# Attention units laid out anew: score bursts, value products, whole-array work and row-half pairs in separate runs

## The chip, the cores and the metric

The kernel runs on one core of one Trainium2 chip. The metric is the device time of one execution in microseconds. A core has TensorE (PE, with its weight loads as PEld), VectorE (DVE), ScalarE (ACT), GpSimd (POOL) and SyncE (SP), which issues most of the DMAs. TensorE writes to PSUM, which has eight banks of 128 x 512 float32 here; GpSimd does not read PSUM in this kernel.

## What is computed

Four layers on one sequence of 2048 rows of width 512, each with a layer norm ahead of it and a residual sum behind it: Fourier mixing, memory attention, Fourier mixing, memory attention.

```
x = x + A(layernorm(x));  x = x + B(layernorm(x));  x = x + A(layernorm(x));  x = x + B(layernorm(x))
A: real part of DFT_seq(DFT_hidden(x)), by given DFT matrices
B: q, k, v = x@wq, x@wk, x@wv  in 32 heads of 16;  four segments of 512 rows, one after the other:
     p = softmax(q k' * scale + causal mask);  a_dot = p v
     phi(t) = t + 1 if t > 0 else exp(t)
     a_mem = (phi(q) M) / (phi(q) z + 1e-6)
     o = g * a_mem + (1 - g) * a_dot,   g = sigmoid(beta) per head
     M += phi(k)' v;  z += sum phi(k)
   result: o @ wo
```

## The kernel before

Every matmul input that needs more than one pass's precision is split in a high and a low part (`split`, L99 to L107: high by ScalarE, low by VectorE or GpSimd), and three passes are summed (`matmul3`). `place_spectral` writes the Fourier layers, `place_attention` the attention layers.

**The order of the work is written out by hand.** Generators are placed on a line of slots: `place(order, gen, times...)` says that the next piece of `gen` runs at each of these times; pieces of the same time run by `order`. All pieces are then issued in that order. TensorE keeps it to the letter (`keep_in_program_order`; its matmuls all stand on L86 of the profile). On the other engines a scheduler orders the instructions by priority; tiles come from pools with a number of buffers (`bufs`), and an instruction that needs a buffer waits until one is free. All PSUM tiles share eight banks (`bank`).

**A unit** is four heads of one segment (`HU` = 4): eight units a segment, 32 an attention, 64 in all. A unit has ten slots; unit n starts at t = t0 + 10 n. The pieces, with their slot in the old layout counted from t (a time of t - 17 is slot 3 of the unit two before):

- `stack` (t - 22): four DMAs on SP (L893) copy q and k of the unit's heads from DRAM (`scrq`, `scrk`) into `stkq` and `stkk`, two heads side by side on the row halves 0 to 63 and 64 to 127. `stkq` has three buffers, and `stkk` is one of three tiles used in turn, so a copy goes over what the unit three before has used last.
- `natural_max` (t - 17, -15, -13, -11, -9, and t - 8): scores in natural order (`nat`, 48 rows on each half of the array), whose row maxima VectorE takes by a fused add-mask-and-minimum (L925, output `junk`); then the maxima are split into `mparts`.
- `max_rows` (t - 5): two transposes (`mT`), two copies by ScalarE (`mt`), two DMAs into spare rows of `stkq` (L963).
- `softmax_values` (t to t + 8): five score bursts, transposed (`sT`, 50 rows on each half): `third` at 0, the two `second` at 2 and 4, the two `first` (512 columns) at 6 and 8. ScalarE rectifies the diagonal blocks (L996) and takes the exponential into `pT` (L999), two of each a burst; GpSimd then zeroes what lies above the diagonal (`affine_select`, L1002).
- `value_products` (t + 11.9): 16 matmuls of 128 rows and 32 columns (`pv_bank`, 32 records of the profile), and a copy by ScalarE (`ot`, L1064).
- `output` (mostly t + 21.9): four transposes (`on`, whole array), a reciprocal, the multiplication (L1105, two halves) and the addition to `o_nat` by GpSimd (L1107).

**Segment items** run on the whole array: `prep` (normalise and transpose rows of the next segment, `xnT` to `xT`; `xn` has two buffers), `transpose_out` (`oT` to `oh`), `mem_read` (`pm`), `mem_update` (transposes `pkT`, a copy `pkn` by ScalarE, then `pM`). `apart(s, k)` puts them at slot 1.9 of the segment's unit k, beside `output` and ahead of `value_products`.

**The chain** holds projections (`pqk`), values (`pvv`) and the output projection (`po`): each tile is 12 products, each done as two half products of 64 rows on the two halves of the array. `chain_step(k)` issues step k of the first half of one tile and step k - `LAG` of the second half of an earlier one, so that two matmuls run side by side (a pair of row halves). A unit holds two tiles, 24 steps, spread evenly:

```
LAG = STEPS * 3 // 2                                     # STEPS = 12
chain_time(k) = t0 + 5 * (k // STEPS) + 2.2 + 4.6 * (k % STEPS) / (STEPS - 1)
```

A tile's second half starts when a score burst behind its first half has been read out of PSUM (`evicted`). `chain_tail` follows the last step: for a projection two copies by ScalarE (`praw`, `parts`), the difference by GpSimd (L855), for phi a rectification and an exponential by ScalarE and a sum by VectorE (`feature_sum`, L851), and two slots later the writes to `scrq` or `scrk` (L869).

Of the kernel before, what the change touches and what calls it, by code (L numbers as in the profile page):

```python
# [19 lines left out]
P = 128  # L20
# [22 lines left out]
HALF = NT // 2  # L43
URGENT = 150
TERMS = {
    "P1": (((0, 1), None, None),),
# [13 lines left out]
def spectral_infini_kernel(  # L60
# [135 lines left out]
    def finish(ps, xr, x_out, i):  # L196
# [5 lines left out]
    spare = v_all.rearrange("p a b -> p (a b)")[:, : 6 * 512].rearrange("p (a b) -> p a b", b=512)  # L202
    v_count = [0]
    max_parts = [
        consts.tile([P, MCOLS], F32R, name=f"mparts{i}") for i in range(2)
# [500 lines left out]
    def place_attention(x_in, x_out, t0, w_at, out_at):  # L706
# [93 lines left out]
        STEPS = DT * len(PASSES)  # L800
        LAG = STEPS * 3 // 2

# [30 lines left out]
        def keep_proj(s, g, n, ps):  # L833
            def phi_tile():
                if (s, g) not in phi:
                    phi[s, g] = pair("phi", "ut", 8, F32)
                return phi[s, g][:, "qk".index(n)]

            parts = sb.tile([P, 2, 512], F32R, name="parts", bufs=2)
            with_phi = (n == "q" and s > 0) or (n == "k" and s < NSEG - 1)  # L840
            late = s == 0 and g < 2
            raw = sb.tile([P, 512], F32, name="praw", bufs=2)
            sign = -1.0 if n == "q" else 1.0

            def feature():
                A.activation(phi_tile(), raw, AF.Relu, scale=-sign)
                A.activation(phi_tile(), phi_tile(), AF.Exp, scale=-1.0)

            def feature_sum():
                op = (ALU.min, ALU.subtract) if n == "q" else (ALU.max, ALU.add)  # L850
                V.scalar_tensor_tensor(phi_tile(), raw, 0.0, phi_tile(), op0=op[0], op1=op[1])  # L851

            A.activation(raw, ps, AF.Copy, scale=sign)
            A.activation(parts[:, 0], ps, AF.Copy, scale=sign)
            G.tensor_tensor(out=parts[:, 1], in0=raw, in1=parts[:, 0].bitcast(F32), op=ALU.subtract)  # L855
# [44 lines left out]
        def natural_max(s, g, u):  # L900
# [3 lines left out]
            def scores(*cols):  # L904
# [16 lines left out]
                for k, (src, dst) in enumerate(views[::2] + views[1::2]):  # L921
                    n = src.shape[1]
                    junk = sb.tile([P, 512], BF16, name="junk", bufs=1)
                    with tc.high_priority(offset=URGENT):
                        last_max[0] = V.tensor_tensor_reduce(  # L925
                            junk[:, :n], src, mask[:, 512 - n :], 1.0, 3e38,
                            ALU.add, ALU.min, dst,
                        )
# [40 lines left out]
        def softmax_values(s, g, u):  # L969
# [60 lines left out]
            for p in range(HP):  # L1030
# [13 lines left out]

                ev(6 + 2 * p, first)
                ev(2 + 2 * p, second)
            p2 = []
# [6 lines left out]

            ev(0, third)

# [10 lines left out]
            pending[s, g, u] = last  # L1067
            for t in range(9):
                for f in events.get(t, ()):
                    f()  # L1070
# [8 lines left out]
        def output(s, g, u):  # L1079
# [16 lines left out]
            for j in range(0, LT, 2):  # L1096
# [180 lines left out]
        def apart(s, k):  # L1277
            return t0 + SS * s + SU * k + 1.9

        for n in range(NSEG * USEG):  # L1280
            t = t0 + SU * n
            final = n >= NSEG * USEG - 2
            place(0, softmax_values(*unit(n)), run_from(t, 9))
# [3 lines left out]
            turn = t - (6 if x_out is out_tiles and n == NSEG * USEG - 1 else 5)  # L1287
            place(1.9, max_rows(*unit(n)), [turn])
            place(1, natural_max(*unit(n)), run_from(t - 17, 5, 2), [t - 8])
            place(0.6, stack(*unit(n)), [t - 22])  # L1290
        for s in range(NSEG):
            b = t0 + SS * s
            for j in range(2):
                t = b - 43 + 5 * j if s == 0 else apart(s - 1, 2 + j)
                first = (12, 10, 6, 4, 3) if s == NSEG - 1 else (11, 8, 5, 3) if s else (8, 5, 4, 3)
                place(0.4, prep(s, (2 * j, 2 * j + 1)), [*(t - d for d in first), t, t + 1] if s == 0 else [*(t - d for d in first), t])
# [4 lines left out]
            order = [chain_proj(s, 3, n) for n in "qk"]  # L1301
            order += [chain_out(s - 1, i) if s else None for i in range(LT)]
# [3 lines left out]
            if s < NSEG - 1:  # L1306
                order += [chain_proj(s + 1, g, n) for g in range(2) for n in "qk"]
                order += [chain_values(s + 1, i) for i in range(2)]
                order += [chain_proj(s + 1, 2, n) for n in "qk"]
                order += [chain_values(s + 1, i) for i in (3, 2)]  # L1310
            chain.update({at + h: tile for h, tile in enumerate(order) if tile})
# [14 lines left out]
            for g in range(NG):  # L1326
# [21 lines left out]
        for j in chain:  # L1348
            end = chain_time(STEPS * (j + 1) - 1 + LAG) + 0.05
            place(2.1, chain_tail(j), [end, end + 1, end + 1.5, end + 2] if chain[j].name == "pqk" else [end])  # L1350
# [110 lines left out]
```

## Time and profile before

| | |
|---|---|
| median of three runs | 1838.15 us (1837.44 to 1843.29) |
| profiled execution | 1843.37 us, span 1841.7 us |
| granted TensorE clock | 0.981 |
| first attention, value products | from 478 to 953 us of the span |
| second attention, value products | from 1384 to 1831 us |

The profile's parts: busy time by engine; groups of instructions (line, engine, operation, output<-input, count, then busy us, mean ns of one, and the idle time before them with what ended it); waits (engine, line, what it waited for: us in total, times, longest); windows (busy time of each engine, with counts, in stretches of the span); the timeline (start in us, time, instructions in order). A matmul's record is longer than its share of the array, since matmuls overlap in the pipe: the pace is read from start to start.

### The profile page before, as it was taken

The page shows a single profiled execution, that of the slowest core. Times are in us where ns is not written, and L with a number is a line of the kernel's source. Part 1 is how long each engine was busy: PE and PEld are TensorE (multiplying, and loading weights), DVE is VectorE, ACT ScalarE, POOL GpSimd, SP SyncE. Part 2 cuts the span into 40 slices and gives each one's busy share as a digit, 9 for nine tenths or more (in the row PEclk, how much of TensorE's full clock was granted, in tenths as well). Part 3 has the DMA queues.
Part 4 walks back from the last instruction along what each step waited for, and adds up shares of the span by engine and source line. Part 5 has one row for each costly group of instructions (what it writes and reads, how often), then busy time and mean ns, then how long its engine had stood idle before and what let it go on. Part 6 is the DMA issues. An engine that isn't in the chain of part 4 may idle for free. (4 is left out here: it accounts for less than half of the span.)

```text
span 1841.7 us, 35419 instructions
## 1 busy us (share of the span) xinstructions
PE 1751.0 (95%) x11504; PEld 1332.9 (72%) x11504; DVE 1389.4 (75%) x4114; ACT 1076.4 (58%) x2452; POOL 362.8 (20%) x673
## 2 busy tenths in 40 slices
PE   8999999999999999999899999999999999989998
PEld 6888777877666666666578878888876667667665
DVE  8888987764766878878867997667457677787784
ACT  3344434441777777677664675453337877767765
POOL 1000000002332333334410000000222333333332
PEclk9999999999899999999799999999998999999988
DMA  7787764354543545544556776645535455455450
GB/s 283 248 268 243 238 222 160 126 166 161 156 132 91 154 124 134 144 123 126 159 189 213 260 237 227 195 134 161 177 117 158 122 134 145 122 133 145 100 133 25
DMA packets 145512, 303.30 MB, mean 165 GB/s; under 512 B 18096, under 2 KB 22192, under 8 KB 145328
## 3 DMA queue, kind: packets, MB, share of 16 engines
q1 hardware_dynamic: 138416, 288.44, 52.8%
q10 hardware_dynamic: 6912, 12.59, 1.8%
q8 instruction: 93, 1.52, 0.4%
q14 instruction: 91, 0.75, 0.1%
HBM read 211.83 MB, written 88.08 MB: 163 GB/s over the span
## 5 line engine op out<-in xcount | busy, mean ns | idle before, releaser
L925 DVE CUSTOM_DVE_ANT_0 junk<-nat,mask 128x512 bf16<-128x512 f32 (+3 forms) x1024 | 499.7, 488 | 172.9 <-PE nat L86 93.9
L999 ACT ACTIVATE pT<-sT 128x512 f32<-128x512 f32 x640 | 354.4, 604 | 0.6 <-POOL pT L1002 0.2
L86 PE MATMUL m<-chi,xa 128*128 128x512 f32 x1056 | 308.7, 392 | 3.1 <-DVE c L549 2.1
L1002 POOL TENSOR_SCALAR_AFFINE_SELECT pT<-pT 128x256 f32<-128x256 f32 (+1 forms) x448 | 195.0, 450 | 513.8 <-ACT pT L999 298.5
L86 PE MATMUL m<-clo,xa 128*128 128x512 f32 x720 | 231.1, 393 | 4.7 <-DVE clo L103 4.4
L86 PEld LDWEIGHTS m<-chi,xa 128*128 128x128 f32 x1056 | 198.0, 189 | 47.5 <-DVE c L549 2.9
L86 PE MATMUL sT<-stkq,stkk 50*128 50x256 f32 (+3 forms) x1024 | 196.0, 356 | 21.8 <-ACT pT L999 17.2
L86 PE MATMUL pqk<-xT,wq 64*128 64x512 f32 (+1 forms) x720 | 214.8, 406 | 0.0
L86 PE MATMUL pqk<-xT,wk 64*128 64x512 f32 (+1 forms) x720 | 208.0, 396 | 0.0
L86 PE MATMUL nat<-stkk,stkq 48*128 48x384 f32 (+3 forms) x1024 | 196.8, 344 | 7.9 <-DVE mx L925 2.6
L996 ACT ACTIVATE sT<-sT 128x256 f32<-128x256 f32 x625 | 181.1, 324 | 38.5 <-PE sT L86 35.5
L86 PE MATMUL pvv<-wv,xT 64*128 64x512 f32 (+1 forms) x672 | 192.7, 405 | 0.0
L86 PEld LDWEIGHTS sT<-stkq,stkk 50*128 50x128 f32 x1024 | 118.4, 189 | 99.7 <-ACT pT L999 33.8
L86 PE MATMUL y<-wdt,us 128*128 128x512 f32 x768 | 182.3, 391 | 0.2 <-DVE wdt L103 0.2
L86 PEld LDWEIGHTS y<-wdt,us 128*128 128x128 f32 x768 | 143.4, 188 | 30.4 <-DVE wdt L103 0.9
L86 PE MATMUL pv_bank<-pT,v_all 128*32 128x512 f32 (+3 forms) x2048 | 160.9, 457 | 3.1 <-DVE mx L925 2.0
L86 PEld LDWEIGHTS nat<-stkk,stkq 48*128 48x128 f32 x1024 | 137.2, 191 | 36.6 <-DVE mx L925 10.3
L86 PEld LDWEIGHTS m<-clo,xa 128*128 128x128 f32 x720 | 135.2, 188 | 37.5 <-DVE clo L103 8.9
L86 PE MATMUL po<-wo,oh 64*128 64x512 f32 (+1 forms) x672 | 155.4, 402 | 0.6 <-ACT oh L101 0.5
L101 ACT ACTIVATE chi<-cring 128x512 fp32r<-128x512 f32 (+1 forms) x138 | 99.6, 727 | 87.6 <-PE m L86 36.7
L1064 ACT ACTIVATE ot<-pv_bank 128x512 f32<-128x512 f32 x64 | 38.4, 601 | 191.1 <-PE pv_bank L86 185.5
L86 PEld LDWEIGHTS pqk<-xT,wk 64*128 64x128 f32 (+1 forms) x720 | 121.2, 187 | 7.9 <-issue 2.2
(187 smaller groups left out, 2940.3 us busy)
## 6 DMA issues: line engine op xcount, KB each, us to landing
cring<-in_ct SPq DMA_DIRECT2D x97, 256.0 KB
scrk<-parts SPq DMA_DIRECT2D x96, 256.0 KB
stkq<-scrq SPq DMA_DIRECT2D x128, 192.0 KB
stkk<-scrk SPq DMA_DIRECT2D x128, 192.0 KB
cring<-sum SPq DMA_DIRECT2D x95, 256.0 KB
xt<-mid SPq DMA_DIRECT2D x64, 256.0 KB
scrq<-parts SPq DMA_DIRECT2D x32, 512.0 KB
cring<-in_ct SPq DMA_DIRECT2D x27, 512.0 KB
```

The lines of the kernel that those rows point to most:

```text
L86: return tc.keep_in_program_order(op(*args, **kwargs))
L101: pin(A.activation(hi, src, AF.Copy, scale=scale))
L925: last_max[0] = V.tensor_tensor_reduce(junk[:, :n], src, mask[:, 512 - n :], 1.0, 3e38, ALU.add, ALU.min, dst,)
L996: done = A.activation(blocks, blocks, AF.Relu)
L999: A.activation(dst[a], ps, AF.Exp, scale=-SCALE)
L1002: G.affine_select(blocks, blocks, pattern=[[0, n] for n in blocks.shape[1:-1]] + [[1, P]], compare_op=ALU.is_ge, fill=0.0, base=0, channel ...
L1064: A.activation(ot[:, 0], pb, AF.Copy)
```

## The change

- **Bursts.** The second `second` moves from slot 4 to 3. `natural_max` moves to t - 17.95, -16.05, -13, -12, -10.9 (slots 2.05, 3.95, 7, 8 and 9.1) and t - 9.
- **Chain.** The 24 steps of a unit lie in three runs: nine from slot 4.1, eight from 6.1, seven from 8.1. `LAG` is 19. The tiles have a new order (before: q3 k3 o0 o1 o2 o3 q0 k0 q1 k1 v0 v1 q2 k2 v3 v2); q0, k0 and so on belong to the next segment.
- **Whole-array work.** Segment items move from 1.9 to 2.5, behind the burst of slot 2 and its maxima; `output` moves to t + 12.5 (also 2.5), nearly a unit earlier. Both `prep` of a segment now stand in its unit 2 (before 2 and 3); the two pieces of `mem_update` stand in units (1, 4, 4, 7) and (2, 5, 7, 8), before both in (1, 4, 5, 7); `mem_read` in (0, 2, 3, 6), before (0, 3, 5, 6).
- **Value products** stay at t + 11.9, now between `third` and the burst of slot 2.
- **Features.** GpSimd clamps `raw` in place and adds it; phi of q has its plain sign, so the memory's denominator adds 1e-6.
- **Maxima.** Two instructions in a row write their unused output to different places: a half of `junk`, or back into PSUM.
- **Output.** For s > 0 one multiplication instead of two.

```diff
+S_AT = (0, 2, 3, 6, 8)
+N_AT = (-17.95, -16.05, -13.0, -12, -10.9, -9)
+PV = 11.9
+W = 2.5
+TO = 0.8
+TURNED = (12.5, 12.5, 14)
+WIN = ((4.1, 9), (6.1, 8), (8.1, 7))
+LAGS = 19
+ORDER = "q3 k3 o0 o1 o2 q0 o3 q1 k0 q2 v0 k1 v1 k2 v3 v2"
+OT_AT = (1, 1, 2, 2)
+PREP_AT = (2, 2)
+READ_AT = (0, 2, 3, 6)
+UPA = (1, 4, 4, 7)
+UPB = (2, 5, 7, 8)
...
-        LAG = STEPS * 3 // 2
+        LAG = LAGS
...
             def feature():
                 A.activation(phi_tile(), raw, AF.Relu, scale=-sign)
                 A.activation(phi_tile(), phi_tile(), AF.Exp, scale=-1.0)
+                G.tensor_scalar(raw, raw, 0.0, None, op0=ALU.max if sign > 0 else ALU.min)
             def feature_sum():
-                V.scalar_tensor_tensor(phi_tile(), raw, 0.0, phi_tile(), op0=op[0], op1=op[1])
+                G.tensor_tensor(
+                    out=phi_tile(), in0=phi_tile(), in1=raw, op=ALU.add if sign > 0 else ALU.subtract
+                )
...
-                    junk = sb.tile([P, 512], BF16, name="junk", bufs=1)
+                    trash = src if n == 512 and k else junk[:, :n] if k % 2 == 0 else junk[:, 512 - n :]
...
-                ev(6 + 2 * p, first)
-                ev(2 + 2 * p, second)
+                ev(S_AT[3 + p], first)
+                ev(S_AT[1 + p], second)
...
-                    V.tensor_tensor(out=tmp, in0=num, in1=rb, op=ALU.mult)
+                    if j == 0:
+                        V.tensor_tensor(
+                            out=tmps,
+                            in0=pn[:, :, :, :DH],
+                            in1=rec.unsqueeze(3).to_broadcast([P, LT, HU, DH]),
+                            op=ALU.mult,
+                        )
...
-                V.tensor_scalar_add(dj, pm[:, :, :, DH], -1e-6)
+                V.tensor_scalar_add(dj, pm[:, :, :, DH], 1e-6)
...
-            return t0 + SS * s + SU * k + 1.9
+            return t0 + SS * s + SU * k + W
...
-            place(0.9, value_products(*unit(n)), [t + (12 if final else 11.9)])
-            turned = t + 14 if n >= NSEG * USEG - 3 else t + 14.5 if n % USEG == USEG - 1 else t + 21.9
-            place(0.5, output(*unit(n)), [turned])
+            place(0.9, value_products(*unit(n)), [t + (PVF if final else PV)])
+            turned = t + TURNED[2 if n >= NSEG * USEG - 3 else n % USEG == USEG - 1]
+            place(TO, output(*unit(n)), [turned])
...
-            place(1, natural_max(*unit(n)), run_from(t - 17, 5, 2), [t - 8])
+            place(1, natural_max(*unit(n)), [t + k for k in N_AT])
             place(0.6, stack(*unit(n)), [t - 22])
...
-                t = b - 43 + 5 * j if s == 0 else apart(s - 1, 2 + j)
+                t = b - 43 + 5 * j if s == 0 else apart(s - 1, PREP_AT[j])
...
-                    place(0.1, transpose_out(s - 1, i), [apart(s, 1 + i // 2)])
+                    place(OWO, transpose_out(s - 1, i), [apart(s, OT_AT[i])])
...
-                    place(0.6, mem_read(s, g), [apart(s, (0, 3, 5, 6)[g])] * 2)
+                    place(OWR, mem_read(s, g), [apart(s, READ_AT[g])] * 2)
...
-                    place(0.3, update, [apart(s, (1, 4, 5, 7)[g])])
-                    place(0.7, update, [apart(s, (1, 4, 5, 7)[g])])
+                    place(OWU, update, [apart(s, UPA[g])])
+                    place(OWB, update, [apart(s, UPB[g])])
         def chain_time(k):
-            return t0 + 5 * (k // STEPS) + 2.2 + 4.6 * (k % STEPS) / (STEPS - 1)
+            u, r = divmod(k, 2 * STEPS)
+            for at, n in WIN:
+                if r < n:
+                    return t0 + SU * u + at + 1.8 * r / n
+                r -= n
```

More of the change, by code (lines that the diff above doesn't have):

```diff
@@ L44 @@
 URGENT = 150
+S_AT = (0, 2, 3, 6, 8)
+N_AT = (-17.95, -16.05, -13.0, -12, -10.9, -9)
+PV = 11.9
+PVF = 12
+W = 2.5
+TURN = -5
+TO = 0.8
[8 more added lines that the diff above has]
+UPB = (2, 5, 7, 8)
+OWO = 0.7
+OWU = 0.3
+OWP = 0.3
+OWR = 0.6
+OWB = 0.85
 TERMS = {
@@ L203, in spectral_infini_kernel @@
     v_count = [0]
+    junk = consts.tile([P, 512], BF16, name="junk")
     max_parts = [
@@ L1053, in third @@
                 causal(t[:, :, :P])
-            ev(0, third)
+            ev(S_AT[0], third)
             def last():
@@ L1067, in softmax_values @@
             pending[s, g, u] = last
-            for t in range(9):
-                for f in events.get(t, ()):
+            for t in sorted(events):
+                for f in events[t]:
                     f()
@@ L1282, in place_attention @@
             final = n >= NSEG * USEG - 2
-            place(0, softmax_values(*unit(n)), run_from(t, 9))
-            place(0.9, value_products(*unit(n)), [t + (12 if final else 11.9)])
-            turned = t + 14 if n >= NSEG * USEG - 3 else t + 14.5 if n % USEG == USEG - 1 else t + 21.9
-            place(0.5, output(*unit(n)), [turned])
-            turn = t - (6 if x_out is out_tiles and n == NSEG * USEG - 1 else 5)
+            place(0, softmax_values(*unit(n)), [t + k for k in sorted(set(S_AT))])
+            place(0.9, value_products(*unit(n)), [t + (PVF if final else PV)])
+            turned = t + TURNED[2 if n >= NSEG * USEG - 3 else n % USEG == USEG - 1]
+            place(TO, output(*unit(n)), [turned])
+            turn = t - (6 if x_out is out_tiles and n == NSEG * USEG - 1 else -TURN)
             place(1.9, max_rows(*unit(n)), [turn])
-            place(1, natural_max(*unit(n)), run_from(t - 17, 5, 2), [t - 8])
+            place(1, natural_max(*unit(n)), [t + k for k in N_AT])
             place(0.6, stack(*unit(n)), [t - 22])
@@ L1293, in place_attention @@
             for j in range(2):
-                t = b - 43 + 5 * j if s == 0 else apart(s - 1, 2 + j)
+                t = b - 43 + 5 * j if s == 0 else apart(s - 1, PREP_AT[j])
                 first = (12, 10, 6, 4, 3) if s == NSEG - 1 else (11, 8, 5, 3) if s else (8, 5, 4, 3)
-                place(0.4, prep(s, (2 * j, 2 * j + 1)), [*(t - d for d in first), t, t + 1] if s == 0 else [*(t - d for d in first), t])
+                place(OWP, prep(s, (2 * j, 2 * j + 1)), [*(t - d for d in first), t, t + 1] if s == 0 else [*(t - d for d in first), t])
             if s == 0:
@@ L1300, in place_attention @@
             at = 2 * USEG * s
-            order = [chain_proj(s, 3, n) for n in "qk"]
-            order += [chain_out(s - 1, i) if s else None for i in range(LT)]
             for i in range(LT):
                 if s > 0:
-                    place(0.1, transpose_out(s - 1, i), [apart(s, 1 + i // 2)])
[L1306 to L1310, printed above, removed]
+                    place(OWO, transpose_out(s - 1, i), [apart(s, OT_AT[i])])
+            order = []
+            for name in ORDER.split():
+                n, i = name[0], int(name[1])
+                if n == "o":
+                    order.append(chain_out(s - 1, i) if s else None)
+                elif n == "v":
+                    order.append(chain_values(s + 1, i) if s < NSEG - 1 else None)
+                elif i == 3:
+                    order.append(chain_proj(s, 3, n))
+                else:
+                    order.append(chain_proj(s + 1, i, n) if s < NSEG - 1 else None)
             chain.update({at + h: tile for h, tile in enumerate(order) if tile})
@@ L1348, in place_attention @@
         for j in chain:
-            end = chain_time(STEPS * (j + 1) - 1 + LAG) + 0.05
+            end = chain_time(STEPS * (j + 1) - 1 + LAG) + 0.01
             place(2.1, chain_tail(j), [end, end + 1, end + 1.5, end + 2] if chain[j].name == "pqk" else [end])
```

3 lines of the change are left out of this document (1 added, 2 removed).

## The prediction

> **What bounds the kernel now.** I read the page, then the windows of the value products for the length of a unit, the waits, and the timelines of TensorE and of the DMA queue around one unit.
>
> ```profile
> span 1841.7 us, 35419 instructions
> PE 1751.0 (95%) x11504; PEld 1332.9 (72%) x11504; DVE 1389.4 (75%) x4114; ACT 1076.4 (58%) x2452; POOL 362.8 (20%) x673
> ```
> ```profile
> 520.00:852.00 332.00, 51.51 (x704) 20.09 (x696) 13.18 (x22) 1.00 0.49 128
> 1424.00:1754.00 330.00, 51.94 (x704) 20.28 (x704) 13.18 (x22) 1.00 0.50 129
> ```
>
> TensorE is the one engine that is nearly always busy. The windows count value products alone: 32 records a unit, so 704 are 22 units, of 15.09 and 15.00 us. About 46 units run with a full chain of row-half pairs; the Fourier stages are not touched. One unit on TensorE, with SyncE's issues beside it:
>
> ```profile
> 1604.78 2.36 PE L86 MATMUL pv_bank<-pT,v_all 128*32 128x512 f32 x32
> ...
> 1607.92 0.50 PE L86 MATMUL nat<-stkk,stkq 48*128 48x512 f32 x2
> ...
> 1609.63 0.66 PE L86 MATMUL on<-ident,ot 128*128 128x128 f32 x4
> ...
> 1611.43 0.40 PE L86 MATMUL pqk<-xT,wq 64*128 64x512 f32 x1
> ...
> 1611.67 0.39 PE L86 MATMUL pqk<-xT,wq 64*128 64x512 f32 x1
> ...
> 1613.30 0.52 PE L86 MATMUL sT<-stkq,stkk 50*128 50x512 f32 x2
> ...
> 1616.54 0.39 PE L86 MATMUL pqk<-xT,wq 64*128 64x512 f32 x1
> 1616.86 1.09 PE L86 MATMUL oT<-ident,onat 128*128 128x128 f32 x8
> 1617.80 0.60 PE L86 MATMUL pkT<-ident,phi 128*128 128x128 f32 x4
> 1619.19 1.20 PE L86 MATMUL pM<-v_all,pkn 128*128 128x136 f32 x8 [0.79 <-ACT pkn L1152]
> 1620.31 2.36 PE L86 MATMUL pv_bank<-pT,v_all 128*32 128x512 f32 x32
> 1622.60 0.50 PE L86 MATMUL sT<-stkq,stkk 50*128 50x384 f32 x4
> 1622.94 0.44 PE L86 MATMUL po<-wo,oh 64*128 64x512 f32 x1
> ...
> 1623.46 0.40 PE L86 MATMUL nat<-stkk,stkq 48*128 48x512 f32 x2
> ```
> ```profile
> 1613.74 0.32 SPq L893 DMA_DIRECT2D stkk<-scrk  x1
> ...
> 1615.05 0.41 SPq L893 DMA_DIRECT2D stkk<-scrk  x1
> ```
>
> The sT of 1613.30 is a unit's last score burst (`first`, p = 1). Starts tell the pace: a pair of row halves every 0.24 us (1611.43 to 1611.67), eight transposes in 0.94 (1616.86 to 1617.80, so 0.47 for four), the value products 2.29 (1620.31 to 1622.60), a burst of four score matmuls 0.34 (1622.60 to 1622.94). Where TensorE waits:
>
> ```profile
> PEld sT L86 <- ACT pT L999: 33.8, 45, 1.1
> PEld mT L86 <- ACT pT L999: 24.3, 43, 1.5
> PE sT L86 <- ACT pT L999: 17.2, 30, 0.6
> PE mT L86 <- ACT pT L999: 16.4, 40, 1.3
> PE pM L86 <- ACT pkn L1152: 12.1, 19, 1.8
> ACT ot L1064 <- PE pv_bank L86: 185.5, 56, 5.5
> ```
>
> It waits for a PSUM bank that ScalarE's exponentials still hold, and in `mem_update` for the copy of its own transposes; ScalarE in turn idles 185.5 us, 3 a unit, under the value products. A wait costs more than its row, for the pipe refills: the unit from 1604.78 to 1620.31 took 15.53 us; without its 0.79 (1.1 with the refill), and with 2.1 us of whole-array work in place of its 2.8 (next part), it would take 13.7. So some 1.35 us of each 15.05 are waits, 62 us in 46 units. That is what new places can take away.
>
> **The change part by part.**
>
> *New places.* Before, a unit ran whole-array work, value products, then bursts with pairs spread evenly. Now: third burst (slot 0), value products (1.9), the burst `second` of p = 0 with the first 512-wide maxima (2, 2.05), whole-array work (2.5), the other `second` with maxima (3, 3.95), nine steps of pairs, burst (6), eight steps with maxima between, burst and maxima (8), seven steps with maxima between. The bursts then lie 2.3 to 2.8 us apart, and one asks ScalarE for two rectifications and two exponentials:
>
> ```profile
> L996 ACT ACTIVATE sT<-sT 128x256 f32<-128x256 f32 x625 | 181.1, 324 | 38.5 <-PE sT L86 35.5
> L999 ACT ACTIVATE pT<-sT 128x512 f32<-128x512 f32 x640 | 354.4, 604 | 0.6 <-POOL pT L1002 0.2
> L925 DVE CUSTOM_DVE_ANT_0 junk<-nat,mask 128x512 bf16<-128x512 f32 (+3 forms) x1024 | 499.7, 488 | 172.9 <-PE nat L86 93.9
> L855 POOL TENSOR_TENSOR parts<-praw,parts 128x512 fp32r<-128x512 f32 x64 | 82.5, 1289 | 100.3 <-ACT parts L854 79.4 <-issue 11.5 <-PE pqk L86 8.3
> L851 DVE SCALAR_TENSOR_TENSOR phi<-praw,phi 128x512 f32<-128x512 f32 x48 | 35.3, 736 | 62.1 <-ACT phi L847 62.1
> ```
>
> 2 x 0.32 + 2 x 0.60 = 1.86 us at most, which fits; and `mem_update`'s second half comes a burst or a unit after its first, so the pkn wait goes. I take the 1.35 us as gone.
>
> *What is late next.* The first 512-wide maxima of unit n+2 need four copies (q and k, both sides) from DRAM, issued at slot 8 when the last burst of unit n-1 frees their buffer:
>
> ```profile
> SPq L893 <- PE sT L86: 14.4, 42, 0.8
> ```
>
> Before, whole-array work and some twelve steps of pairs lay between; 1613.30 to 1623.46 is 10.16 us. Now the whole-array work lies behind the maxima and seven steps are between: burst 0.24 (two 512-wide parts run as a pair does), maxima 0.34, seven steps 1.68, maxima 0.34, third burst 0.34, a mode change 0.2, value products 2.29, burst 0.34: 5.8 us. The trace has one unit near the end of the second attention that already runs in nearly that order, with few pairs left:
>
> ```profile
> 1775.76 0.39 PE L86 MATMUL sT<-stkq,stkk 50*128 50x512 f32 x1
> ...
> 1781.83 0.47 PE L86 MATMUL nat<-stkk,stkq 48*128 48x512 f32 x1 [0.36 <-ACT ot L1064]
> 1783.61 0.47 PE L86 MATMUL nat<-stkk,stkq 48*128 48x512 f32 x1 [1.31 <-DMA stkk<-scrk]
> ```
> ```profile
> 1776.75 0.38 SPq L893 DMA_DIRECT2D stkk<-scrk  x1
> ...
> 1778.11 0.41 SPq L893 DMA_DIRECT2D stkk<-scrk  x1
> ```
>
> There TensorE stood still for the last copy, 6.86 us behind the first issue. With 0.44 from burst to issue (1613.30 to 1613.74) I take 7.3 us from the last burst to the second maxima, in every unit; ends: 5.8 (copies never late) and 7.85 (1775.76 to 1783.61). I lean to 7.3 as it joins a usual issue with the one landing that a wait shows. Behind the waiting matmul stand the whole-array work and all later bursts; ScalarE and GpSimd use the time to catch up, so their small delays before it cost nothing.
>
> *The other half of the loop*, maxima to last burst: 1607.92 to 1613.30 is 5.38. Take out the "on" group in it with its two mode changes (0.47 + 2 x 0.2), add five steps of pairs (17 instead of 12; 5 x 0.24), two mode changes (0.4) and the whole-array work. A segment of eight units has 20 groups of four transposes (8 on, 4 oT, 4 xnT, 4 pkT) of 0.47, and 8 of pm or pM:
>
> ```profile
> 1681.76 0.93 PE pm L86 x8
> 1682.69 0.93 PE pM L86 x8
> ```
>
> 20 x 0.47 + 8 x 0.93 = 16.8, or 2.1 a unit. Sum: 5.38 - 0.87 + 1.2 + 0.4 + 2.1 = 8.2. The loop is 7.3 + 8.2 = 15.5 against 15.05: **+0.45 x 46 = +21 us**. The new wait eats what the old ones gave.
>
> *Mode changes.* From pairs to whole array a start comes 0.32 us after the last (1616.54 to 1616.86) where it would be 0.12: 0.2 us. A unit had three changes (pairs, whole array, value products, scores); now four. All four stand in the loop above; the added one alone is 46 x 0.2 = 9 us. The Trainium skill, "TensorEngine Tiling (Array Packing)", Key Properties, says that changing the tiling mode drains TensorE, and so speaks against this change: the trace's 0.2 us agrees, and by that rule alone, every wait unchanged, the time would be 9 us longer, 1847.
>
> *Segment items.* Both `prep` of a segment now come in one slot, with two buffers for four normalised rows, so the second pair of rows is normalised only when the first is transposed: twice some 0.7 us of VectorE in TensorE's way, less what the old units with these items lost: 0 to 2 us, taken 1.2, six times: +7. In the new order k of group 0 ends at slot 5.3 of a segment's sixth unit; its three writes are issued at 7.31, just ahead of the copies at slot 8 that read them (before, 6.7 slots ahead of them). SyncE's queue then stands on GpSimd's difference (1.29), and the copies behind it: 0 to 3 us, taken 1, six times: +6. The one hole more in the first segment's chain is under 1 us.
>
> *Units without a full chain* (some ten at the attentions' ends) have ScalarE and VectorE as their limit; evener bursts give up to 2 us each: taken -10.
>
> *GpSimd.* 48 times VectorE loses 0.74 us, and GpSimd gains a clamp, bounded by the row of a 512-wide mask and L855 (0.64 to 1.29), and a sum of 1.29: 93 to 124 us on an engine busy 363 of 1842. Behind them in its queue stand the causal masks, and the value products behind these. Cover: TensorE would wait 1.5 us for the copies anyway (7.3 - 5.8). Without it, up to 1 us in 48 places. Cost taken: nothing.
>
> ```profile
> 1575.46 0.64 POOL L1002 TENSOR_SCALAR_AFFINE_SELECT pT<-pT 128x512 f32<-128x512 f32 x1 [1.23 <-ACT pT L999]
> ```
>
> *Scratch of the maxima, one multiplication for two in `output`, 1e-6, LAG 19:* VectorE's gaps between its 16 maxima a unit shrink (172.9 - 93.9 us idle over 1024 is at most 0.08 each); at 75% it is no limit. The lag holds a bank one step (0.24) longer. Nothing.
>
> Sum: 21 + 7 + 6 - 10 = **+24 us** on the profiled execution's 1843.37 us (span 1841.7 and what lies around it): 1867. That execution lay 5.2 above the median 1838.15 of the runs, so 1862 there.
>
> **The rivals.**
>
> *Faster: the copies land in time.* If the path from last burst to maxima is 5.8 and ScalarE's lateness leaves 0.4 a unit, the loop is 14.4: 46 x -0.65 = -30, -10 for the ends, +7 for the `prep` items: 1805. For it: only 1.3 us of TensorE's time in the whole trace waits on a copy. Against it: that is where the order was like the new one. It decides at 6.85 us from burst to maxima, where the loop equals 15.05; at 6.55 the sum is -11 and the time 1827.
>
> *Even (within 0.3%, 5.5 us, about what this measurement can tell from no change).* The old waits and the new one weigh the same: 6.7 to 6.9 us from burst to maxima, 1838.
>
> *Slower still: GpSimd.* The masks wait behind clamp and sum by more than the copies hide: 48 x 1 us more than 1862, 1910. Against: 20% busy, and value products that hardly wait for it now.
>
> **How the numbers follow.** Slower by the copies 0.47, slower by GpSimd as well 0.07; even 0.12; faster 0.34. The likeliest case alone runs from 6.9 to 7.85 us, 1844 to 1887. The range of all, 1800 (below the faster rival's 1805) to 1890, leaves out the GpSimd rival and the far ends of the others, under 2 in 10.
>
> **What would show it.** Right: a TensorE wait "nat <- DMA stkk" or "stkq" of 1 to 2 us a unit (50 to 90 us in all), units of 15.3 to 15.7; waits for pkn gone, those of sT and mT for pT mostly so; VectorE 35 us less busy, GpSimd some 110 more. Wrong: no such wait, units of 14.5 or less; or value products that wait for POOL pT.

## Result and the profile after

The changed kernel takes 1964.28 us (median of 1945.68 to 1968.14) against 1837.8 in the same comparison: ratio 1.066 [1.059, 1.073], 126 us slower. The forecast was 1862. The profiled execution is the one of 1968.14 us; its mean granted clock is 0.935, before 0.981.

The page of the changed kernel: span, busy time by engine, and the granted clock in 40 slices.

```profile
span 1966.4 us, 35346 instructions
PE 1832.3 (93%) x11504; PEld 1426.4 (73%) x11504; DVE 1344.3 (68%) x4018; ACT 1096.3 (56%) x2452; POOL 488.3 (25%) x769
PEclk9999999999799999889899999999978988988988
```

TensorE is busy for 81 us more with as many matmuls (11504), so its records themselves are longer, and it is idle for 43 us more (span less busy time: 134 against 91): the two make up the 125 us of the span. The slices with 7 and 8 lie in the attentions. The clock records in these traces hold full and half clock and nothing between. The stretches at half clock sum to 70 us before and 256 after, and the means say the same: twice the shortfall times the span is 2 x 0.019 x 1841.7 = 70 and 2 x 0.065 x 1966.4 = 256. I call this sum the half-clock time; the table below has it for each run from the records, and the sum from the means lies within 3 us of it.

The windows of the value products (length, PE, PEld, ACT, then clock, DMA share, GB/s):

```profile
541.00:899.00 358.00, 50.18 (x672) 19.79 (x672) 12.63 (x21) 0.92 0.44 115
1481.00:1868.60 387.60, 52.16 (x708) 20.39 (x711) 13.25 (x22) 0.89 0.43 110
```

358 us are 21 units of 17.05 us, 387.6 are 22.1 of 17.5, where before they took 15.09 and 15.00, and the clock is 0.92 and 0.89 where it was 1.00. The mean hides a wide spread: from start to start of the value products, the units of these windows take 13.9 to 23.1 us.

The waits of VectorE, the DMA queue and TensorE (us in total, times, longest):

```profile
DVE junk L949 <- PE nat L107: 257.9, 145, 13.2
SPq L917 <- PE nat L107: 50.2, 44, 2.9
PE nat L107 <- DMA stkk<-scrk: 65.1, 47, 2.3
PE nat L107 <- DMA stkq<-scrq: 15.5, 15, 2.4
PEld nat L107 <- ACT pT L1023: 55.6, 46, 2.5
PE xnT L107 <- DVE xn L214: 6.3, 4, 2.2
PEld sT L107 <- ACT pT L1023: 20.5, 47, 0.7
```

Gone are the waits for `pkn` and those of `mT` for `pT`. New are 81 us in which the maxima (`nat`) wait for the copies (65.1 + 15.5; before 1.3), and 55.6 us in which their weight loads wait for ScalarE (before 3.8). The line of the queue (SPq) is about the issue of the copies: they now wait 50.2 us for maxima, where before they waited 14.4 us for the last burst (shown in the prediction) and 4.9 for maxima.

One unit on TensorE, with SyncE's issues of its copies:

```profile
692.04 2.36 PE L107 MATMUL pv_bank<-pT,v_all 128*32 128x512 f32 x32
694.33 0.50 PE L107 MATMUL sT<-stkq,stkk 50*128 50x384 f32 x4
695.54 0.47 PE L107 MATMUL nat<-stkk,stkq 48*128 48x512 f32 x1 [0.71 <-DMA stkq<-scrq]
697.79 0.46 PE L107 MATMUL nat<-stkk,stkq 48*128 48x512 f32 x1 [1.78 <-DMA stkk<-scrk]
698.18 1.92 PE L107 MATMUL pm<-state,phi 128*128 128x136 f32 x8
699.89 1.06 PE L107 MATMUL on<-ident,ot 128*128 128x128 f32 x4
700.88 0.80 PE L107 MATMUL sT<-stkq,stkk 50*128 50x384 f32 x4
...
709.65 2.36 PE L107 MATMUL pv_bank<-pT,v_all 128*32 128x512 f32 x32
```
```profile
690.88 0.32 SPq L917 DMA_DIRECT2D stkk<-scrk  x1
...
692.18 0.41 SPq L917 DMA_DIRECT2D stkk<-scrk  x1
```

The second maxima start 6.91 us behind the first issue. The forecast had 6.86: this step is right to 0.05 us. What follows was not forecast. The eight `pm` take 1.71 us from start to start (698.18 to 699.89), before 0.93; the four `on` take 0.99, before 0.47. The windows of the same stretch show why (PE, PEld, DVE, ACT, POOL; then the granted clock); the two rows below them take the stretch by the edges of the clock record:

```profile
694.00:696.00 2.00, 1.29 (x13) 0.48 (x5) 0.00 (x0) 1.99 (x6) 1.92 (x2) 1.00 0.99 166
696.00:698.00 2.00, 0.22 (x2) 0.18 (x1) 0.70 (x2) 0.61 (x2) 1.49 (x4) 1.00 0.98 293
698.00:700.00 2.00, 2.00 (x10) 1.82 (x10) 0.93 (x3) 0.00 (x0) 0.00 (x0) 0.62 0.27 102
700.00:702.00 2.00, 1.95 (x12) 1.46 (x10) 1.47 (x9) 0.23 (x1) 0.00 (x0) 0.52 0.00 0
702.00:704.00 2.00, 2.00 (x19) 1.81 (x21) 1.88 (x10) 1.64 (x6) 1.41 (x4) 1.00 0.00 0
```
```profile
695.08:698.49 3.41, 1.17 (x4) 0.68 (x5) 0.90 (x3) 1.53 (x4) 2.41 (x4) 1.00 0.95 262
698.50:701.90 3.40, 3.38 (x17) 2.87 (x15) 2.09 (x12) 0.13 (x1) 0.00 (x0) 0.50 0.02 8
```

TensorE stands nearly still for 3 us (0.22 us of work from 696 to 698), and the granted clock is then half for 3.41 us; the 0.62 and 0.52 are means over its edges. So the wait is paid a second time, in the work behind it. The Trainium skill, "TensorE: Matmul & The Clock Gate", Part 1, says that an idle window of about 3.4 us halves the clock and that about as much steady work restores it. The trace agrees on the length, and shows that the window need not be wholly idle: in the 3.41 us ahead of this drop TensorE was busy for 1.17. Of the 42 half-clock stretches of this trace, 38 begin behind 3.41 us in which TensorE was busy for two thirds or less.

### The profile page after: what moved, and what is told of

Read it like the earlier page. It is cut to its first block, busy times and chain, and to the rows that moved or that the text cites. A ratio compares the mean times of both kernels' runs of the same rounds, so it can differ in the third digit from the quotient of the medians.

```text
span 1966.4 us, 35346 instructions
## 1 busy us (share of the span) xinstructions
PE 1832.3 (93%) x11504; PEld 1426.4 (73%) x11504; DVE 1344.3 (68%) x4018; ACT 1096.3 (56%) x2452; POOL 488.3 (25%) x769
## 4 chain that ended last, share of the span: by engine, by line
PE 70%; DMA 14%; DVE 8%; ACT 3%; issue 3%; SPq 2%; POOL 0%; ACTq 0%; DVEq 0%; POOLq 0%
PE m L107 22%; DMA stkk<-scrk 13%; PE pqk L107 9%; PE y L107 7%; PE nat L107 6%; PE po L107 5%; PE pvv L107 4%; PE sT L107 4%; PE u L107 4%; PE pv_bank L107 3%; PE on L107 2%; PE pm L107 2%; DVE clo L124 2%; DVE c L571 2%; SPq L917 2%
## 5 line engine op out<-in xcount | busy, mean ns | idle before, releaser
L949 DVE CUSTOM_DVE_ANT_0 junk<-nat,mask 128x128 bf16<-128x128 f32 (+3 forms) x896 | 369.7, 458 | 283.0 <-PE nat L107 257.9
L107 PE MATMUL nat<-stkk,stkq 48*128 48x384 f32 (+3 forms) x1024 | 220.6, 378 | 98.4 <-DMA stkk<-scrk 65.1
L107 PEld LDWEIGHTS nat<-stkk,stkq 48*128 48x128 f32 x1024 | 136.1, 205 | 139.7 <-ACT pT L1023 55.6
L107 PE MATMUL pqk<-xT,wk 64*128 64x512 f32 (+1 forms) x720 | 197.7, 409 | 0.0
L107 PE MATMUL pqk<-xT,wq 64*128 64x512 f32 (+1 forms) x720 | 192.3, 428 | 0.7 <-ACT pT L1023 0.7
L107 PE MATMUL sT<-stkq,stkk 50*128 50x256 f32 (+3 forms) x1024 | 186.7, 366 | 3.4 <-DVE onat L1167 0.8
L107 PE MATMUL pvv<-wv,xT 64*128 64x512 f32 (+1 forms) x672 | 164.2, 425 | 0.0
L107 PEld LDWEIGHTS sT<-stkq,stkk 50*128 50x128 f32 x1024 | 114.3, 204 | 60.6 <-ACT pT L1023 20.5
L107 PEld LDWEIGHTS pqk<-xT,wk 64*128 64x128 f32 (+1 forms) x720 | 130.7, 198 | 12.7 <-issue 2.0
L193 POOL TENSOR_TENSOR r<-ve,half_neg 128x2 f32<-128x2 f32 (+2 forms) x24 | 19.6, 818 | 474.5 <-DVE ve L191 446.5
```

The costliest lines, as they stand in the source:

```text
L107: return tc.keep_in_program_order(op(*args, **kwargs))
L193: G.tensor_tensor(out=r, in0=ve, in1=half_neg[:, :n], op=ALU.pow)
L949: last_max[0] = V.tensor_tensor_reduce(trash, src, mask[:, 512 - n :], 1.0, 3e38, ALU.add, ALU.min, dst,)
```

## The experiments

All are timed in turn with the kernel before (1838.6 to 1840.9 us beside these runs); each ratio is to it. The last column sums the waits of TensorE's matmuls; in e7 and e2 weight loads wait for the copies too, 32 and 16 us, in part under the idle pairs.

| run | kernel | us | ratio [95%] | half-clock us | maxima wait for copies, us |
|---|---|---|---|---|---|
| before | | 1838 | 1 | 70 | 1 |
| after | | 1964 | 1.066 [1.059, 1.073] | 256 | 81 |
| e1 | after, first maxima one slot later | 1849 | 1.005 [1.004, 1.007] | 93 | 9 |
| e7 | after, 4 idle pairs ahead of the maxima | 1907 | 1.037 [1.035, 1.040] | 80 | 38 |
| e2 | after, 8 idle pairs | 1913 | 1.040 [1.038, 1.042] | 48 | 15 |
| e3 | after, old tile order and preps | 1923 | 1.045 [1.042, 1.048] | 164 | 53 |
| e4 | after, sums on VectorE | 1967 | 1.072 [1.066, 1.078] | 243 | 80 |
| e5 | e1 + e3 | 1857 | 1.011 [1.008, 1.014] | 107 | 3 |
| e6 | e5, `mem_read` as before | 1860 | 1.012 [1.010, 1.014] | 127 | 2 |
| e8 | e1, items spread | 1852 | 1.007 [1.006, 1.008] | 124 | 6 |
| b1 | before, maxima in the new order | 1915 | 1.041 [1.039, 1.043] | 124 | 22 |
| b2 | before, `mem_update` parted | 1828 | 0.995 [0.994, 0.997] | 60 | 3 |
| b3 | b2 + two places for unused output | 1807 | 0.983 [0.982, 0.985] | 53 | 3 |
| b4 | b3 + sums on GpSimd, one multiplication | 1815 | 0.987 [0.984, 0.990] | 53 | 2 |
| e9 | after, whole-array work ahead | 1851 | 1.007 [1.005, 1.009] | 107 | 18 |
| e10 | e9 + pairs spread | 1834 | 0.996 [0.994, 0.998] | 77 | 10 |
| e11 | e10 + e3 | 1824 | 0.990 [0.988, 0.992] | 82 | 7 |
| e12 | e11, `transpose_out` and `mem_read` spread | 1829 | 0.993 [0.991, 0.996] | 76 | 4 |

**e1: the first maxima one slot later, behind the whole-array work.**

```diff
-N_AT = (-17.95, -16.05, -13.0, -12, -10.9, -9)
+N_AT = (-16.95, -16.05, -13.0, -12, -10.9, -9)
```

> The new kernel with its first 512-wide maxima at slot 3.05 instead of 2.05, behind the whole-array work and the other second burst. Copies theory (TensorE waits in every unit for the copies of q and k, and the granted clock falls after such waits): the waits of nat for stkk and stkq, 81 us in the new kernel, go to under 15 us, the half-clock time from 256 us to under 130, and the time from 1964 to 1800-1850. Items theory (the piled-up prep unit, the late k of group 0 and GpSimd's queue cost most of the 126 us): under 40 us less, 1925 or more.

1849.46 us, the slow end of what the copies theory expected: one constant gives back 115 of the 126 us. Its windows and waits:

```profile
520.00:852.00 332.00, 52.30 (x704) 21.22 (x704) 13.23 (x22) 0.97 0.49 126
1424.00:1754.00 330.00, 52.03 (x704) 20.19 (x704) 13.27 (x22) 0.98 0.49 128
```
```profile
PE nat L107 <- DMA stkk<-scrk: 6.9, 9, 2.1
PE xnT L107 <- DVE xn L214: 11.4, 8, 2.6
```

22 units in the same 332 and 330 us as before; quiet ones take 13.3 to 14.6 us, and the first units of a segment, with its items, 17 to 21. So the place of these maxima makes the loss, by wait or by clock.

**e2 and e7: fill the wait.** Eight (e2) or four (e7) pairs of row-half matmuls of no use ahead of the first 512-wide maxima, into the same banks, which the maxima then overwrite.

```diff
+                if cols == ((0, 3),):
+                    for _ in range(IDLE):                 # 8, or 4
+                        for a, at in enumerate(SIDES):
+                            T.matmul(banks[a], w[at : at + P // 2, 0, :P],
+                                     w[at : at + P // 2, 0, :], start=True, stop=True)
```

> The new kernel with eight idle pairs of row halves (16 matmuls of 512 columns on resident weights, results overwritten) ahead of the first 512-wide maxima of each unit: 1.85 us of added TensorE work at the place where it waits for the copies. Clock theory (half of the 126 us is the granted clock that falls to half after TensorE stood still): half-clock time falls from 256 us to under 130 and the time falls in spite of the added work, to 1880-1920. Plain waiting (the clock is not what counts): the added work is hidden or adds up to 40 us, 1960-2005.

> As e2, with four idle pairs of row halves instead of eight (0.93 us of added TensorE work a unit). Clock theory: part of the stand-still is filled; half-clock time between 48 us (eight pairs) and 256 us (none), and a time between or below 1913 and 1964, I expect 1900-1930. If the gain of e2 came from something that eight pairs did by their length (a later order of everything behind), four give half of it or less: 1935-1955.

A pair costs 0.23 us, so e2 adds 1.85 us of work to each of 64 units, 118 us in all, and is 51 us *faster* than the changed kernel; e7 adds half and is 57 us faster. The waits of e7, then of e2:

```profile
PE nat L108 <- DMA stkk<-scrk: 33.5, 47, 1.6
```
```profile
PE nat L108 <- DMA stkk<-scrk: 13.2, 18, 1.5
PE nat L108 <- DMA stkq<-scrq: 2.0, 2, 1.4
```

The wait alone explains none of this: work put into a wait can at best cost nothing. The half-clock time falls from 256 to 80 and 48 us. With e2's clock kept at 0.988, what is left above before is 75 us: the wait (now filled), the items and filler that outlasts the wait, in shares that these runs don't part. So the clock is shown to be worth at least the 57 us of e7, since filler can shorten nothing by itself; how much more is not shown.

**e3, e4: the other suspects, undone on the changed kernel.** e3 takes back the tile order and puts the two `prep` in units 2 and 3; e4 takes the feature sums back to VectorE.

> The new kernel with the chain's old order of tiles (o3 before q0, q0 k0 q1 k1 in a row) and the two prep items in units 2 and 3 as before. Items theory: the segments' heaviest units (22 us) fall to 17, k of group 0 is in time again, 40-80 us less, 1890-1925. Copies theory: the waits in the other units stay, 15-35 us less, 1930-1950.

> The new kernel with the feature sums back on VectorE (one instruction instead of two on GpSimd, phi of q with its minus sign again). Copies theory: off the path, within 10 us of 1964. GpSimd theory (the causal masks and with them the value products stand behind clamp and sum): 30 us less or more.

e3 gives 41 us, but with 27 us less waiting for the copies and 92 us less at half clock. e4 gives nothing (1967.13): in the changed kernel GpSimd's sums are covered.

**e5, e6, e8: the same and other spreads on e1.** e5 is e1 with e3's edit; e6 moves `mem_read` to units (0, 3, 5, 6) besides; e8 is e1 with `transpose_out`, `mem_read` and the second half of `mem_update` spread.

> The new kernel with both edits together: first 512-wide maxima at slot 3.05, old order of the chain's tiles and prep in units 2 and 3. In e1 the units without a wait take 13.3 to 14.2 us, and what is left lies in the segments' heavy units (17 to 21 us). If these come from both preps in one unit, 20-45 us less than e1: 1805-1830, faster than before. If they come from ScalarE and VectorE being late after any whole-array run, 0-10 us less: 1840-1850.

> As the run before, with mem_read in units 0, 3, 5, 6 as in the old kernel instead of 0, 2, 3, 6, so that unit 2 holds eight whole-array matmuls less. Pile-up theory: a further 3-10 us less. If only the number of such items counts: within 5 us of the run before.

> e1 (maxima behind the whole-array work) with less in unit 2 of each segment: one transpose_out in unit 3, mem_read of group 1 in unit 3, the second half of mem_update of group 0 in unit 3, so 20 whole-array groups fewer by 16 matmuls there. Pile-up theory: e1's units of 17 to 21 us shrink by some 2-3 us each, six times: 1825-1840, at or below the kernel before. If the two preps alone make the pile: within 6 us of e1 (1849).

1856.64, 1859.58 (ratio 1.012 [1.010, 1.014]) and 1851.92 us: none is faster than e1. What e3 gave came by the wait and the clock, and it is gone once the wait is.

**b1: the order alone, in the old layout.** The first maxima at t - 17.95, and whole-array work and `output` just behind them; bursts, chain and items stay.

```diff
-            return t0 + SS * s + SU * k + 1.9
+            return t0 + SS * s + SU * k + 2.1
...
-            turned = ... else t + 21.9
+            turned = ... else t + 22.1
-            place(1, natural_max(*unit(n)), run_from(t - 17, 5, 2), [t - 8])
+            place(1, natural_max(*unit(n)), [t - 17.95], run_from(t - 15, 4, 2), [t - 8])
```

> The kernel before with one thing of the change alone: its first 512-wide maxima at slot 2.05 and the whole-array work at 2.1 behind them (output at t + 22.1), pairs, bursts and chain as they were. Copies theory: the path from last burst to maxima falls from about 9 to about 6.5 us, nat waits for stkk or stkq in most units (20-50 us in all), half-clock time rises above 100 us, and the time to 1860-1900. If one mode change more is all it costs (0.2 us a unit): 1842-1852.

1915.09 us, more than the 1860 to 1900 expected: this order alone costs 76 us in a kernel that has nothing else of the change. Its waits:

```profile
PE nat L86 <- DMA stkk<-scrk: 20.8, 30, 1.7
PEld nat L86 <- DVE mx L925: 23.8, 31, 2.0
```

They sum to less than the loss; 54 us more stand at half clock.

**b2, b3, b4: the small parts alone, in the old layout.** b2 puts the second half of `mem_update` a unit later, (2, 5, 6, 8); b3 adds the two places for the maxima's unused output; b4 adds GpSimd's sums and the single multiplication.

```diff
-                    place(0.7, update, [apart(s, (1, 4, 5, 7)[g])])
+                    place(0.7, update, [apart(s, (2, 5, 6, 8)[g])])
```

> The kernel before with the second half of mem_update one unit after the first, as in the change, and nothing else. Before, TensorE waits 12.1 us (pM for pkn) and its weight loads 17.0. If such a wait is worth its row and the refill: 10-20 us less, 1820-1830. If the next wait in the unit takes it up: within 5 us of 1838.

> b2 with the maxima's unused output written to two places in turn, as in the change. VectorE's gaps shrink; it is 75% busy and not the limit: within 4 us of b2. If VectorE sets the bank releases that TensorE waits for: 5-20 us less than b2.

> b3 with the two other small edits of the change, feature sums on GpSimd and one multiplication in output, in the old layout. Cover theory: VectorE is relieved of 35 us, GpSimd's queue is 20% busy: 0-8 us less than b3's 1807. GpSimd theory: the causal masks come late and the value products wait, as nothing else covers them here: 10-45 us more.

b2 gives 10 us (1828.34). b3 gives 21 more, just beyond the 5 to 20 expected: 1807.17, **0.983 [0.982, 0.985], the fastest kernel of this study, 31 us faster than before**. Its maxima, as groups of instructions:

```profile
L926 DVE CUSTOM_DVE_ANT_0 junk<-nat,mask 128x128 bf16<-128x128 f32 (+3 forms) x896 | 370.8, 458 | 158.0 <-PE nat L86 144.0 <-PE mT L86 4.5 <-PE pqk L86 2.3
L926 DVE CUSTOM_DVE_ANT_0 nat<-nat,mask 128x512 f32<-128x512 f32 x128 | 88.8, 694 | 1.5 <-PE sT L86 1.1 <-PE nat L86 0.3
```

The 1024 maxima keep VectorE busy for 459.6 us together (370.8 + 88.8) where they took 499.7, though 128 of them now write a whole float32 row back to PSUM. A single maximum is no shorter (896 x 458 and 128 x 694 ns make 488 on average, as before); two in a row now overlap. Two of 512 columns on VectorE, in b2, then in b3:

```profile
607.02 0.69 DVE L925 CUSTOM_DVE_ANT_0 junk<-nat,mask 128x512 bf16<-128x512 f32 x1
...
607.86 0.69 DVE L925 CUSTOM_DVE_ANT_0 junk<-nat,mask 128x512 bf16<-128x512 f32 x1
```
```profile
604.21 0.69 DVE L926 CUSTOM_DVE_ANT_0 junk<-nat,mask 128x512 bf16<-128x512 f32 x1
...
604.83 0.69 DVE L926 CUSTOM_DVE_ANT_0 nat<-nat,mask 128x512 f32<-128x512 f32 x1
```

From start to start 0.84 us become 0.62. In b2 the trace has the second wait for a semaphore that VectorE itself raises behind the first, which writes the same place; in b3 this pair has no such wait. Of the 1024 maxima 941 wait for VectorE's own semaphore in b2, 352 in b3. That reaches TensorE by the banks; its three largest waits for these maxima in b2, then the same in b3:

```profile
PEld nat L86 <- DVE mx L925: 13.5, 20, 1.8
PEld sT L86 <- DVE mx L925: 12.8, 33, 1.1
PE nat L86 <- DVE mx L925: 6.2, 10, 1.4
```
```profile
PEld sT L86 <- DVE mx L926: 8.0, 15, 2.1
PEld nat L86 <- DVE mx L926: 4.5, 9, 0.7
PE nat L86 <- DVE mx L926: 1.0, 3, 0.4
```

32.5 us become 13.5; with all its smaller waits for maxima, 53 become 31, about the 21 us of the whole. b4 loses 8 us (1815.42), where one theory expected a small gain and the other a loss of 10 or more; the intervals of the two ratios overlap a little, so the 8 us are barely told from none. Its group of clamps:

```profile
L849 POOL TENSOR_SCALAR praw<-praw 128x512 f32<-128x512 f32 x48 | 72.3, 1505 | 3.0 <-POOL parts L858 0.5 <-ACT phi L847 0.5
```

A clamp takes 1.51 us, more than the forecast's upper bound of 1.29.

**e9 to e12: what else the new layout costs.** In e9 the whole-array work and `output` move ahead of the value products, so the maxima stay where the change put them and the copies have the time of the whole-array work again; e10 spreads the pairs evenly as before besides, with `LAG` 18; e11 takes e3's edit on top; e12 also puts `transpose_out` in units (0, 1, 1, 2) and `mem_read` in (0, 3, 5, 6).

```diff
-W = 2.5
+W = 1.9
-TO = 0.8
-TURNED = (12.5, 12.5, 14)
+TO = 0.5
+TURNED = (21.9, 14.5, 14)
...                                                         # e10:
+            return t0 + 5 * (k // STEPS) + 2.2 + 4.6 * (k % STEPS) / (STEPS - 1)
...                                                         # e11:
+ORDER = "q3 k3 o0 o1 o2 o3 q0 k0 q1 k1 v0 v1 q2 k2 v3 v2"
+PREP_AT = (2, 3)
```

> The new kernel with the whole-array work ahead of the value products again (slot 1.9, output at t + 21.9), all else new, the first maxima at 2.05. The path from last burst to maxima holds the whole-array work again. Copies theory: waits of nat for the copies under 30 us, half-clock time under 130. Place theory (whole-array work between two bursts costs e1 its 42 us, by a fourth mode change and by what ScalarE and VectorE are late there): 1805-1830. Otherwise 1840-1870, and the three runs of pairs are left.

> As e9, with the chain's pairs spread evenly over the unit as before (LAG 18): of the new layout only the places of the bursts and maxima, the order of the tiles and the items' units are left. Runs theory (three runs of pairs cost the 42 us): 1805-1825 and at least 15 us below e9. Otherwise within 10 us of e9.

> The whole-array work ahead of the value products and the pairs spread (e10, 1834 us), now with the tile order of before and one prep a unit (units 2 and 3). Theory A, the two preps in one unit are what is left of the loss: the six units of 21.6 to 28.4 us among others of 13.5 to 14.5 fall to 16 or 17 and their neighbours rise by some 2, 6 x 5 = 30 us less, about 1803, below the two small edits on the old layout (1807). Rival, as when the same was undone on the maxima one slot later (1849 to 1857): the time for xn and the row statistics is lost in two units instead of one, 1826 to 1842.

> The same, and the segment items transpose_out in units 0, 1, 1, 2 and mem_read in units 0, 3, 5, 6 as well, so that unit 2 holds one transpose_out beside prep and unit 3 holds the second prep. Theory A': unit 2 still does too much on VectorE (two oh copies beside the row statistics), so spreading gives 5 to 10 us more than the run before it. Rival: the items' units don't matter, as on the maxima one slot later (1857 to 1860): within 4 us of the run before it.

e9 takes 1851.33 us, as e1 does: it matters that the whole-array work lies between the last burst and these maxima, not on which side of the value products. e10 takes 1833.52: the three runs of pairs cost 18 us beside the even spread with its lag, though the 1805 to 1825 expected were not reached. In its trace most units take 13.5 to 14.5 us, and the units with two `prep` in the second and third segment of each attention 21.6 to 28.4. Here is the end of one of 24.0 us on TensorE:

```profile
723.52 0.66 PE L107 MATMUL xnT<-ident,xn 128*128 128x128 f32 x4
725.49 1.09 PE L107 MATMUL xnT<-ident,xn 128*128 128x128 f32 x8 [1.31 <-DVE xn L214]
728.29 0.63 PE L107 MATMUL xnT<-ident,xn 128*128 128x128 f32 x4 [1.71 <-DVE xn L214]
```

Two waits of 1.31 and 1.71 us for `xn`, whose buffers come free only as the transposes are done. They are part of the excess: earlier in the same unit a burst waits 1.50 us for VectorE's maxima and another 1.05 for ScalarE. In e11 those units take 18.4 and 19.8 us, and the whole 1823.93: 10 us better, a third of what was expected, the rest moved to neighbours of 15.5. e12 gains nothing more (1828.90).

## Why the forecast was wrong in size

*The new wait: right.* Its place and its cause are as forecast; 81 us lie between the 50 and 90 named. e1 and b1 show that it is the place that does it.

*The step that failed is the sum of the loop, "The loop is 7.3 + 8.2 = 15.5 against 15.05".* Both of its terms came out larger. The timelines give them as averages over the units with a full chain (the 4th to 26th of each attention, 46 in all). In e2 the idle pairs lie within the second row, and the third row includes the two `prep`, which the forecast priced apart (7 us, 0.15 a unit):

| us | forecast | before | after | e2 |
|---|---|---|---|---|
| last burst to first issue of the copies | 0.44 | 0.79 | 1.05 | 1.07 |
| first issue to second maxima | 6.86 | 9.11 | 6.90 | 7.16 |
| second maxima to last burst | 8.2 | 5.19 | 9.44 | 8.28 |
| loop | 15.5 | 15.1 | 17.4 | 16.5 |

The larger miss is the 8.2, by 1.2 us in each of 46 units, 57 us. It prices the work behind the wait by rows of a trace in which TensorE hardly ever stood still. In the changed kernel that work runs in part at half clock; in e2, where idle pairs keep the clock up and this part of the loop is otherwise the same, it takes 8.28, nearly the forecast. That the clock belongs to the cause is also shown by the times: the idle pairs shorten the kernel by adding work, by 51 and 57 us. The 186 us more at half clock could be worth up to 93 us of TensorE's work, but that is a ceiling, not a measurement. The other miss is in the 7.3: the time from issue to maxima is right to 0.04 us, but the 0.44 from burst to issue was read in one unit, while the trace of before has 0.79 on average and the changed kernel 1.05. That is 28 us in 46 units, and it isn't the clock, for e2 has it too; what holds up the issue is open, beyond the queue's waits for maxima (50.2 us). The units of 15.3 to 15.7 named as a sign came out at 17.05 and 17.5.

*"I take the 1.35 us as gone": wrong in sum.* The waits for `pkn` and of `mT` and `sT` for `pT` did mostly go. But ScalarE's exponentials now hold the banks that the maxima need: 55.6 us of weight loads waiting in 46 places, partly under the wait for the copies. And where the copies hardly disturb, the average unit still doesn't come down to the 13.7 us: 15.2 in e1 and 14.8 in e10, against 15.06 before. Quiet units do (13.3 to 14.6 in e1), but they hold less whole-array work than the average that the 13.7 was worked out for.

*The ends of the attentions, taken as -10: wrong.* From the 27th value products to the last, the two attentions took 81.6 and 60.1 us before and take 81.5 and 69.0 after. No run was made for this term.

*Both `prep` in one slot, "twice some 0.7 us", six times 1.2: too small.* In the changed kernel such a unit takes up to 23.1 us, in e10 up to 28.4. Parting them gives 10 us in e10 and nothing on e1, so the net price lies near the forecast's 7; what failed is where it lies, with waits of up to 2.6 us for `xn` in e10 and not 0.7. The late k has no run of its own, but the queue's waits show it: copies wait 14.2 us in 15 places for k's write to land, against 3.7 in 3 before, where 6 us were taken.

*GpSimd: right in the changed kernel, by its cover.* e4 shows no difference. Without the cover it costs some 8 us (b4 against b3, with the multiplication, barely clear of noise), which the forecast put at up to 48.

*"Scratch of the maxima ... Nothing": wrong.* The forecast spread the idle time over all maxima, at most 0.08 us each. Between two in a row that write the same place it was 0.15 (607.71 to 607.86 in b2), and without the wait the second also starts before the first ends: 0.22 us a pair of 512 columns, 40 us of VectorE's busy time, 21 us of the whole (b2 to b3). That VectorE is 75% busy was no reason, since its maxima hold PSUM banks for which TensorE waits (53 us of such waits in b2, 31 in b3).

*VectorE and GpSimd:* 45 us less and 126 more busy, against 35 and 110. The 45 are not the sums alone: b3 loses 43 us without moving any.

*The rivals.* The copies came late in nearly every unit, so the faster rival fell; that its 1805 is about what b3 reaches by other means is chance. The even and the GpSimd rival fell too.

*Still open:* between e11 and b4, which has the same small edits in the old layout, are 9 us, from the places of bursts, value products and items. No run parts these. How much of the loss is clock and how much is wait can't be split exactly, as each run that changes one changes the other; at least 57 us for the clock is what the idle pairs show.

## What to carry over

Price a new wait twice: once for itself, and once for the work behind it if the standstill is long enough to lower the granted clock; read the clock row of the window behind a stall. Read a term of the sum in all units and not in one. When a transfer's buffer is freed by the last work of a loop, keep the work that depends on nothing between that point and the transfer's first reader; here one constant was worth 115 us. Take a change apart: two small parts of it, alone, were faster than the whole and than the kernel before.

## What was not expected of the hardware

- About 3 us of TensorE standing nearly still, with 1.17 us of work in the 3.41 us ahead, are followed by 3.41 us at half clock; over the kernel 256 us at half clock against 70. Useless matmuls that keep TensorE busy through the wait save 51 to 57 us.
- Two maxima in a row that write their unused output to one place start 0.84 us apart (512 columns), since the second waits for VectorE's own semaphore; with two places they overlap and start 0.62 apart, and the kernel gains 21 us. Each alone is as long as before.
- GpSimd's clamp of 128 x 512 float32 in place takes 1.51 us, longer than its sum of two such tiles (1.30 in the same run).
